# One more column group of a GEGLU layer by seven products, with its LayerNorms moved

## The chip, the core and the metric

The kernel runs on one core of one Trainium2 chip. The metric is the time of one execution on the device in microseconds, the median of several runs. TensorE (PE) multiplies matrices, VectorE (DVE), ScalarE (ACT) and GpSimd (POOL) work element by element, SyncE (SP) issues nearly all DMAs. Each engine takes its own instructions strictly in the order written, and waits where an operand is not there yet.

## The reference

The layer takes `x` (2048 rows of 640) and computes, in float32, attention and a feed-forward part, each behind a LayerNorm and each added to its input:

```
h   = x + attention(layernorm(x))            # 32 heads of 20, window of 256 rows
h2  = h + (gelu(n @ w_gate) * (n @ w_up)) @ w_down      with n = layernorm(h)
```

`w_gate` and `w_up` are 640 x 1536, `w_down` is 1536 x 640. The change concerns the second line alone.

## The kernel before

**Tiling.** The rows are cut into 16 blocks of 128, and for the feed-forward part into four chunks of 512 rows (chunk 0 to 3). The 1536 columns of `w_gate` and `w_up` are cut into three column groups of 512 (group 0 to 2), and a group into four tiles of 128 columns. Every float32 operand is split into two float16 parts, high and low (`hh`, `hl` for the rows; `w5h`, `w5l` and so on for weights: `gu` and w5, w6 hold the gates of groups 0, 1, 2; `gu`, w8, w9 the ups; w10, w11, w12 the downs), and a product of two such operands is three float16 products summed: high by high, high by low, low by high.

**Order of the groups.** `ORDER` (L1061) lists pairs (chunk, group): (0,0), (1,0), (0,1), (0,2), (1,1), (1,2), then the three groups of chunk 2 and of chunk 3. The first `PLAIN` (L1063) pairs are made by `gate_up` (L1104): for each of the four tiles, five contraction steps of three products of 512 columns for the gate, and as many for the up. The result of a tile goes through GELU, is multiplied (`gel`), and split again into `ah` and `al` (`gate_out`, L1087). `down` (L1219) then multiplies the four tiles of a pair by the down weights in eight halves of twelve products of 320 columns, and VectorE adds each half to the accumulator `ht` (`down_out`, L1233). Plain pairs and `down` share two PSUM banks named mm.

**The seven products.** The remaining pairs are made by `quad` (L1135). It shares work between gate and up and between the two halves of 256 rows of a chunk in the manner of a fast matrix multiplication, so that for the low parts seven block products of 128 by 256 do for eight; beside them are the two high-by-high products of 512 columns. It needs sums of the rows (`token_sums`, L1289, twenty VectorE instructions for a chunk, tile `ts` or `wst`) and sums of the weights (`weight_sums`, L1314: for each tile two instructions on POOL and two on VectorE, tile `ws` with two buffers). The weight sums of a group are computed the first time that it is needed, stored to DRAM (`wsums`) and loaded in later chunks (`QLOAD`). A tile takes one bank tp, one of ra, one pv, one of rb, put together by `quad_out` (L1172) on ScalarE, POOL and VectorE. Between two tiles come two halves of the `down` of the pair before.

**Weights.** The feed-forward weights come through one buffer, `wst`, one after another in the order gate, up, down of each group: load, VectorE's maximum, a scale, the split into high and low, and only then the next load.

**LayerNorm.** Chunk 0 is normalised during attention (`first_norm_lane`, L1338) from the block `ht`, into a tile `lxn`, and transposed on TensorE. Chunks 1 to 3 are read back from DRAM (`h_dram`) into two buffers `wsl` by two lanes h and i, a block at a time (`norm_start` and `norm_lane`, L1266 and L1277), normalised there, split, and transposed by DMA into `hT` (`turned`, L499). Chunk 2 uses chunk 0's `hT` tiles and chunk 3 those of chunk 1, so `norm_start` waits until all three groups of the chunk two before have been issued.

**What sets the order.** A planner in the kernel (`Clock`, L54, and the loop at L1561) runs generators called lanes and writes every engine's instructions in the order in which it believes that they become ready, by its own costs; lanes for the outputs of matmuls come ahead of side lanes (weights, sums, LayerNorm), each with a bound on how far ahead it may be written (`FFBACK`, L296). The order on an engine is fixed when the kernel is built. All operations are recorded under one line, L199, so tiles and not lines tell them apart.

Of the kernel before, what the change touches and what calls it, by code (L numbers as in the profile page):

```python
# [11 lines left out]
F32 = mybir.dt.float32  # L12
# [9 lines left out]
S, D, H, DH, F = 2048, 640, 32, 20, 1536  # L22
P = 128
NB = S // P
KC = D // P
# [4 lines left out]
FG = 3  # L30
# [19 lines left out]
def _pow2(e):  # L50
    return float(2.0 ** e)
# [202 lines left out]
def block_kernel(ctx: ExitStack, tc: tile.TileContext, x, wqkv, wo, wg, wu, wd, out):  # L254
    nc = Clock(tc.nc)
# [4 lines left out]
    lnp = ctx.enter_context(tc.tile_pool(name="lnp", bufs=2))  # L260
# [6 lines left out]
    opened, pos = Counter(), Counter()  # L267
# [25 lines left out]
    OUT, PREP, RAMPMAX, FFPREP, LATE = 0.75, 0.55, 0.25, 0.2, 0.4  # L293
# [8 lines left out]
    def need(*reads, slots=(), when=None, eng="tensor"):  # L302

        def f():
            if when and not when() or any(opened[n] >= banks[n] for n in slots):
                return INF
            return max([nc.ready(reads, eng)]
                       + [nc.slot(psum, n, banks[n]) for n in slots])
        return f

    def pe(*reads, slots=(), when=None):
        return ("tensor",), need(*reads, slots=slots, when=when)

    def on(eng, *reads, when=None, after=None):
        f = need(*reads, when=when, eng=eng)
        if after is not None:
            return (eng,), lambda: max(f(), nc.others(after, eng))
        return (eng,), f
# [132 lines left out]
    W = {}  # L451
# [9 lines left out]
    def layernorm(xt, lane, hi, lo, dst=None, when=None, xn=None, e=XE, tp="tp",  # L461
                  dma=False):

        T = lambda n, *shape: nc.tile(lnp, [P] + list(shape), F32, n + lane)
        st = T("lst", 2, 6)
        for i in range(2):
            yield on("vector", xt)
            nc.vector.bn_stats(st[:, i, :], xt[:, i * 320:(i + 1) * 320])
        yield on("vector", st)
        mv = T("lmv", 2)  # L470
        nc.vector.bn_aggr(mv, st)
        yield on("vector", mv)
        ve = T("lve", 1)
        nc.vector.tensor_scalar(ve, mv[:, 1:2], EPS, None, op0=ALU.add)
        yield on("gpsimd", ve)

        y = T("ly", 1)
        a = T("lya", 1)
        nc.gpsimd.tensor_tensor(y, ve, mhalf, op=ALU.pow)
        yield on("vector", y)  # L480
        nc.vector.scalar_tensor_tensor(a, y, ve, y, op0=ALU.mult, op1=ALU.mult)
        yield on("vector", a)
        nc.vector.tensor_scalar(a, a, -0.5 * _pow2(e), 1.5 * _pow2(e), op0=ALU.mult, op1=ALU.add)
        yield on("vector", a)
        nc.vector.tensor_tensor(y, y, a, op=ALU.mult)
        yield on("vector", y)
        xn = xn()
        nc.vector.tensor_scalar(xn, xt, mv[:, 0:1], y, op0=ALU.subtract, op1=ALU.mult)
        if dma:
            yield from turned(xn, lane, (hi, lo), dst, when)  # L490
            return
        yield pe(xn, slots=[tp], when=when)
        if dst:
            hi, lo = dst()
        yield from transpose_part(xn, hi, lo, 0, 4, tp)
        yield pe(xn, slots=[tp])
        yield from transpose_part(xn, hi, lo, 4, 5, tp)
# [84 lines left out]
    gu = ffw.tile([P, 4 * KC * 512], F16, name="gu")  # L582
# [3 lines left out]
    gu = gu.rearrange("p (a c f) -> p a c f", c=KC, f=512)  # L586
# [52 lines left out]
    def hpart(c, b):  # L639
        return tuple(t[:, :, b * P:(b + 1) * P] for t in hT[c])  # L640
# [12 lines left out]
    B = [Block() for _ in range(NB)]  # L653
# [406 lines left out]
    NCH = S // (CB * P)  # L1060
    ORDER = [(0, 0), (1, 0), (0, 1), (0, 2), (1, 1), (1, 2)]  # L1061
    ORDER += [(c, fg) for c in range(2, NCH) for fg in range(FG)]
    PLAIN = 4  # L1063
    hts, ga = {}, {}
    ffpools = [None, None]

# [197 lines left out]
    lnbuf = []  # L1264

    def norm_start(c):  # L1266
        yield ("sync",), need(when=lambda: pos["gu", c - 2] == FG if c > 1 else (
            ffpools[0] and W["d", 0].ready and all(b.wrote for b in B[CB:2 * CB])), eng="sync")
        if c == 1:
            hT[1] = tuple(nc.tile(ffpools[0], [P, KC, CB * P], F16, n) for n in ("h1h", "h1l"))  # L1270
            lnbuf.extend(nc.tile(stage, [P, D], F32, "wsl", SLICES) for _ in range(3))
        else:
            hT[c] = hT[c - 2]
        for i, n in enumerate("hi"):
            side.append((LATE, norm_lane(c, (i, i + 2), n, lnbuf[i])))

    def norm_lane(c, bs, lane, t):  # L1277
        for b in bs:
            j = c * CB + b
            yield ("sync",), lambda: nc.others(t, "sync")  # L1280
            nc.sync.dma_start(t, h_dram[j * P:(j + 1) * P, :])
            yield from layernorm(t, lane, *hpart(c, b), xn=lambda: t, dma=True)
            chunk[c] += 1
        if chunk[c] == CB:
            side.append((LATE, token_sums(c)))
# [3 lines left out]
    def token_sums(c):  # L1289
        hh, hl = hT[c]  # L1290
        h1, h2 = hh[:, :, :CW], hh[:, :, CW:]
        l1, l2 = hl[:, :, :CW], hl[:, :, CW:]
        yield on("vector", when=lambda: ffpools[1] and (c == 1 or W["d", FG - 1].ready))
        t = (nc.tile(ffp, [P, KC, 512], F32, "ts") if c % 2 else
             nc.tile(ffpools[0], [P, KC, 512], F32, "wst")).bitcast(F16)
        t = t.rearrange("p c (a n) -> p a c n", a=4)
        for ks in (slice(k, k + 1) for k in range(KC)):
            a, b, m, d = (t[:, i, ks] for i in range(4))
            yield on("vector", h1, h2)
            nc.vector.tensor_tensor(a, h2[:, ks], h1[:, ks], op=ALU.subtract)  # L1300
            yield on("vector", a, l2)
            nc.vector.scalar_tensor_tensor(b, a, -_pow2(-TE), l2[:, ks], op0=ALU.mult, op1=ALU.add)
            yield on("vector", b, l1)
            nc.vector.tensor_tensor(d, l1[:, ks], b, op=ALU.subtract)
            yield on("vector", l2, h2)
            nc.vector.scalar_tensor_tensor(m, l2[:, ks], _pow2(TE), h2[:, ks], op0=ALU.mult,
                                           op1=ALU.subtract)
        TS[c] = t

    WS = {}  # L1310
    QLOAD = [(c, fg) for c in range(2, NCH) for fg in range(FG) if (c, fg) != (2, 0)]
    wsums = dram.tile([FG * FT, P, 4 * KC * P], F16, name="wsums")

    def weight_sums(c, fg, ft):  # L1314
        kept = wsums[fg * FT + ft]
        t = nc.tile(ffp, [P, 4, KC, P], F16, "ws", 2)
        flat = t.rearrange("p a c f -> p (a c f)")
        if (c, fg) in QLOAD:
            yield ("sync",), need(kept, eng="sync")
# [18 lines left out]
    def first_norm_lane():  # L1338

        for b in range(CB):  # L1340
            yield on("vector", when=lambda: B[b].halves == 2)
            yield from layernorm(B[b].h, "h", *hpart(0, b),
                                 xn=lambda: nc.tile(lnp, [P, D], F32, "lxn"))
            B[b].normed = True
            chunk[0] += 1


    later = [(kind, fg) for fg in range(FG) for kind in "gud"]
# [113 lines left out]
    ffp = None  # L1462
# [5 lines left out]
    def feed_forward():  # L1468
        quads = [(c, fg, ft) for c, fg in ORDER[PLAIN:] for ft in range(FT)]

        def sums_lane():
            for i, q in enumerate(quads):
                yield on("gpsimd", when=lambda: pos["quads"] >= i - 1 and W["d", 2].ready)
                yield from weight_sums(*q)

        side.append((LATE, sums_lane()))
        sums["r", 0] = nc.tile(ffp, [P, 2, CW], F32, "rr")
        sums["r", 1] = nc.tile(ffpools[0], [P, CB * P], F32, "gelt").rearrange(
            "p (a n) -> p a n", a=2)
        sums["s"] = nc.tile(ffp, [P, 3, CW], F32, "rs")  # L1480
        prev = None
        for c, fg in ORDER[1:PLAIN]:
            yield from gate_up(c, fg)
            if prev:
                yield from down(*prev)
            prev = (c, fg)
        for c, fg in ORDER[PLAIN:]:
            groups = down(*prev)

            def fill():  # L1490
                for _ in range(2):
                    for y in groups:
                        if y is None:
                            break
                        yield y

            pool = ffpools[ORDER.index((c, fg)) % 2]
            ga[c, fg] = tuple(nc.tile(pool, [P, FT, CB * P], F16, n) for n in ("ah", "al"))
            for ft in range(FT):
                yield from quad(c, fg, ft, fill)  # L1500
            pos["gu", c] += 1
            prev = (c, fg)
        yield from down(*prev)
# [48 lines left out]
    side = [(LATE, g) for g in lanes]  # L1552
# [91 lines left out]
```

## Time and profile before

| what | before |
|---|---|
| median of three runs | 1042.01 us (1041.12 to 1042.12) |
| profiled execution, its own time | 1043.35 us |
| its span on the core | 1041.6 us |
| TensorE busy | 1019.7 us, 98% of the span |
| VectorE, ScalarE, POOL busy | 778.4, 490.6, 269.8 us |
| granted TensorE clock, mean over the span | 0.996 |

Times in the rows below are microseconds from the start of the span. A row of the chain or of the timeline is start, duration, engine, line, and what was written from what; `x3` is a count, and `[2.00 <-DVE gel L199]` is idle time ahead of the instruction and the one that ended it. A row of a table by stages gives the stage, its length, the busy time of each engine with the count of its instructions, the granted clock, the share of the DMA engines and their rate. Matmuls overlap, so their pace is read from one start to the next.

By the trace, attention ends at about 613 us. Pair (1,0) starts at 619.3, (0,1) at 646.1, `down` of (1,0) at 672.2, (0,2) at 686.0, `down` of (0,1) at 712.5, the first pair by seven products, (1,1), at 729.4. Each of the eight pairs by seven products takes some 37 us together with the `down` work between its tiles; the `down` of the last pair closes the kernel.

### The profile page before, as it was taken

What the parts mean: (1) busy time and instruction counts of PE and PEld (TensorE: products, weight loads), DVE (VectorE), ACT (ScalarE), POOL (GpSimd) and SP (SyncE); (2) the same over time, 40 slices, a digit from 0 to 9 for tenths busy, and PEclk for the clock granted to TensorE, in tenths of its full rate; (3) what the DMA queues carried; (4) which work ended last, traced back from release to release, by engine and by line L of the source; (5) the groups of instructions that cost most, each with busy time, mean ns of one, the idle gap of its engine ahead of it and who ended that gap; (6) DMA issues with size and microseconds to landing.
All of it is one profiled execution on the core that took longest, in us unless ns stands there. A gap on an engine that the chain in (4) does not pass through costs nothing.

```text
span 1041.6 us, 26895 instructions
## 1 busy us (share of the span) xinstructions
PE 1019.7 (98%) x10802; PEld 691.2 (66%) x10802; DVE 778.4 (75%) x2193; ACT 490.6 (47%) x938; POOL 269.8 (26%) x369
## 2 busy tenths in 40 slices
PE   8999999999999999999999899999999999999998
PEld 7876567667666666676655564555777777777776
DVE  6878989998787777677687867676997985445553
ACT  6512667666666766666667835341122222222220
POOL 7100332233333323232323511031445310000000
PEclk9999999999999999999999999999999999999999
DMA  8663354361341513415302341314342652122211
GB/s 300 149 133 114 119 121 132 122 150 55 73 107 43 101 45 77 77 44 112 129 28 90 78 139 52 101 51 127 102 144 110 164 166 77 59 94 102 77 51 51
DMA packets 89116, 105.86 MB, mean 102 GB/s; under 512 B 22176, under 2 KB 63392, under 8 KB 88992
## 3 DMA queue, kind: packets, MB, share of 16 engines
q1 hardware_dynamic: 76896, 93.41, 31.2%
q10 hardware_dynamic: 12096, 10.75, 3.2%
q8 instruction: 84, 1.38, 0.6%
q14 instruction: 40, 0.33, 0.1%
HBM read 71.11 MB, written 28.84 MB: 96 GB/s over the span
## 4 chain that ended last, share of the span: by engine, by line
PE 78%; DVE 13%; issue 3%; DMA 3%; ACT 2%; POOL 0%; SPq 0%; DVEq 0%; ACTq 0%
PE mm L199 40%; PE pv L199 11%; PE ra L199 11%; PE rb L199 9%; PE tp L199 7%; DVE junk L199 4%; DMA qT<-qk 1%; DVE am L199 1%; DMA wst<-in_wd_dram 1%; DVE m L199 1%; DVE al L199 0%; DVE ht L199 0%; ACT pt L199 0%; DVE qks L199 0%; DMA wsl<-h_dram 0%
## 5 line engine op out<-in xcount | busy, mean ns | idle before, releaser
L199 POOL TENSOR_SCALAR_AFFINE_SELECT pt<-pt 128x512 f32<-128x512 f32 x240 | 152.9, 659 | 361.4 <-ACT pt L199 358.7
L199 DVE CUSTOM_DVE_ANT_0 junk<-rb,mask 128x384 bf16<-128x384 f32 (+2 forms) x262 | 138.9, 530 | 42.4 <-PE rb L199 22.6
L199 DVE CUSTOM_DVE_ANT_0 junk<-ra,mask 128x384 bf16<-128x384 f32 (+2 forms) x250 | 132.2, 529 | 41.4 <-PE ra L199 22.3
L199 ACT ACTIVATE pt<-ra,esc 128x384 f32<-128x384 f32 (+2 forms) x248 | 130.7, 579 | 68.4 <-PE ra L199 57.3
L199 ACT ACTIVATE pt<-rb,esc 128x384 f32<-128x384 f32 (+2 forms) x232 | 122.0, 578 | 70.1 <-PE rb L199 59.2
L199 PE MATMUL pv<-pt,v 128*21 128x128 f32 x2880 | 104.8, 277 | 2.1 <-ACT oT L199 2.1
L199 PEld LDWEIGHTS <-ah 128*128 128x128 f16 x768 | 75.5, 98 | 31.1 <-issue 3.1
L199 ACT ACTIVATE gel<-gel,ffk 128x512 f32<-128x512 f32 x32 | 23.1, 722 | 121.4 <-DVE gel L199 121.4
L199 PEld LDWEIGHTS pv<-pt,v 128*21 128x21 f32 x2880 | 68.8, 101 | 17.0 <-ACT oT L199 2.8
L199 PEld LDWEIGHTS <-kT 62*128 62x128 f16 x1440 | 57.8, 95 | 22.7 <-issue 12.7
L199 PEld LDWEIGHTS <-ws 128*128 128x128 f16 x640 | 62.6, 98 | 7.2
L199 PEld LDWEIGHTS <-gu 128*128 128x128 f16 x440 | 42.1, 98 | 36.6 <-issue 1.5
L199 ACT CAST ah<-gel 128x512 f16<-128x512 f32 x48 | 29.6, 616 | 75.7 <-DVE gel L199 75.7
L199 DVE SCALAR_TENSOR_TENSOR ht<-mm,ffk,ht 128x320 f32<-128x320 f32 x96 | 51.9, 545 | 15.9 <-PE mm L199 13.8
L199 PEld LDWEIGHTS <-qT 60*128 60x128 f16 x640 | 24.5, 93 | 56.7 <-issue 55.3
L199 PE MATMUL mm<-xh,w1h 128*128 128x256 f16 x200 | 54.6, 273 | 1.6 <-DVE qks L199 1.6
L199 PE MATMUL mm<-xl,w1h 128*128 128x256 f16 x200 | 54.7, 273 | 0.0
L199 PE MATMUL mm<-xh,w1l 128*128 128x256 f16 x200 | 54.7, 273 | 0.0
L199 PE MATMUL mm<-w3h,oh 128*128 128x320 f16 x160 | 48.0, 300 | 0.1
L199 PE MATMUL mm<-w2h,xh 128*128 128x320 f16 x160 | 48.1, 300 | 0.0
L199 PE MATMUL mm<-w3l,oh 128*128 128x320 f16 x160 | 48.0, 300 | 0.0
L199 PE MATMUL mm<-w2h,xl 128*128 128x320 f16 x160 | 48.0, 300 | 0.0
(296 smaller groups left out, 2531.8 us busy)
## 6 DMA issues: line engine op xcount, KB each, us to landing
ws<-wsums SPq DMA_DIRECT2D x20, 640.0 KB
qk<-qks ACTq DMA_DIRECT2D x32, 256.0 KB
qT<-qk SPq DMA_DIRECT2D x48, 160.0 KB
kT<-qk SPq DMA_DIRECT2D x48, 160.0 KB
wsums<-ws SPq DMA_DIRECT2D x12, 640.0 KB
ht<-in_x_dram SPq DMA_DIRECT2D x16, 320.0 KB
h_dram<-ht SPq DMA_DIRECT2D x16, 320.0 KB
ht<-h_dram SPq DMA_DIRECT2D x16, 320.0 KB
```

Source lines behind the costliest of these rows:

```text
L199: r = real(*args, **kw)
```

## The change

Four edits belong together.

1. `PLAIN` is 3 for 4: pair (0,2) is made by `quad`. Its weight sums (group 2) are now the first to be computed, those of (1,1) come second, and (1,2) loads group 2's from DRAM where it computed them before. Twelve tiles of sums are computed and stored as before; 24 are loaded for 20. The lane of weight sums waits for its own group's gate and up weights, where it waited for the last down weights (`W["d", 2]`).
2. Chunk 0 gets row sums of its own (`token_sums(0)`, tile `ts0`), twenty VectorE instructions, which can start when attention has ended.
3. `norm_start` for chunks 2 and 3 goes when two groups of the chunk two before have been issued, not three: the first block of each of the two lanes is loaded and normalised one group sooner. Only the split and the transposes wait for the third group (`when` in `norm_lane`).
4. The LayerNorm of chunk 0 writes over `ht` itself, and the tile `lxn` goes.

```diff
-    PLAIN = 4
+    PLAIN = 3
...
-        yield ("sync",), need(when=lambda: pos["gu", c - 2] == FG if c > 1 else (
+        yield ("sync",), need(when=lambda: pos["gu", c - 2] == FG - 1 if c > 1 else (
             ffpools[0] and W["d", 0].ready and all(b.wrote for b in B[CB:2 * CB])), eng="sync")
...
-            yield from layernorm(t, lane, *hpart(c, b), xn=lambda: t, dma=True)
+            yield from layernorm(t, lane, *hpart(c, b), xn=lambda: t, dma=True,
+                                 when=lambda: c < 2 or pos["gu", c - 2] == FG)
...
-        yield on("vector", when=lambda: ffpools[1] and (c == 1 or W["d", FG - 1].ready))
-        t = (nc.tile(ffp, [P, KC, 512], F32, "ts") if c % 2 else
+        yield on("vector", when=lambda: ffpools[1] and (c < 2 or W["d", FG - 1].ready))
+        t = (nc.tile(ffp, [P, KC, 512], F32, "ts" if c else "ts0") if c % 2 or not c else
              nc.tile(ffpools[0], [P, KC, 512], F32, "wst")).bitcast(F16)
...
-    QLOAD = [(c, fg) for c in range(2, NCH) for fg in range(FG) if (c, fg) != (2, 0)]
+    QLOAD = [q for i, q in enumerate(ORDER) if q[1] in [fg for _, fg in ORDER[PLAIN:i]]]
...
             yield from layernorm(B[b].h, "h", *hpart(0, b),
-                                 xn=lambda: nc.tile(lnp, [P, D], F32, "lxn"))
+                                 xn=lambda: B[b].h)
             B[b].normed = True
             chunk[0] += 1
+        side.append((LATE, token_sums(0)))
...
-                yield on("gpsimd", when=lambda: pos["quads"] >= i - 1 and W["d", 2].ready)
+                yield on("gpsimd", when=lambda: pos["quads"] >= i - 1 and W["g", q[1]].ready
+                         and W["u", q[1]].ready)
```

## The prediction

> **What bounds the kernel now.** I read the page's busy shares first, then the table by stages, then what TensorE waits for, then the chain, and last the timeline where the chain leaves TensorE.
>
> ```profile
> PE 1019.7 (98%) x10802; PEld 691.2 (66%) x10802; DVE 778.4 (75%) x2193; ACT 490.6 (47%) x938; POOL 269.8 (26%) x369
> ```
>
> TensorE is busy 98% of the span, so what is left to win is a little work and a few waits. The stages show where (span from:to, then busy time of PE, PEld, DVE, ACT, POOL, the granted clock, DMA):
>
> ```profile
> 620.00:646.00 26.00, 25.84 (x122) 11.88 (x121) 19.76 (x49) 11.04 (x17) 2.91 (x3) 1.00 0.32 113
> 646.00:674.00 28.00, 28.00 (x136) 13.22 (x135) 18.59 (x34) 12.52 (x20) 4.60 (x4) 1.00 0.29 95
> 674.00:686.00 12.00, 11.92 (x88) 8.37 (x86) 8.29 (x21) 4.62 (x7) 2.32 (x2) 1.00 0.21 61
> 686.00:716.00 30.00, 28.23 (x136) 13.13 (x135) 20.04 (x34) 9.76 (x14) 9.89 (x7) 1.00 0.24 87
> 716.00:730.00 14.00, 13.71 (x90) 9.46 (x90) 10.78 (x28) 2.07 (x3) 1.10 (x2) 0.88 0.40 95
> 730.00:767.00 37.00, 37.00 (x279) 27.05 (x278) 35.17 (x64) 6.79 (x11) 14.89 (x12) 1.00 0.30 99
> ```
>
> From 730 on TensorE has no idle time: such stages move only if TensorE has less to do. Before, in 686 to 730, it lacks 2.1 us of 44, and in the second of these two stages the granted clock is 0.88, where the other rows have 1.00. The chain passes there through a DMA, and the rows of SP, VectorE and TensorE around it tell the story:
>
> ```profile
> 707.74 4.19 DMA wsl<-h_dram
> ```
> ```profile
> 665.57 2.23 SPq L199 DMA_DIRECT2D wst<-in_wu_dram  x5
> 682.35 2.23 SPq L199 DMA_DIRECT2D wst<-in_wd_dram  x4
> 702.68 5.02 SPq L199 DMA_DIRECT2D wsums<-ws  x2
> 707.74 1.38 SPq L199 DMA_DIRECT2D wsl<-h_dram  x2
> ```
> ```profile
> 711.95 0.89 DVE L199 BATCH_NORM_STATS2 lsth<-wsl 128x6 f32<-128x320 f32 x2 [3.52 <-DMA wsl<-h_dram]
> ...
> 715.50 0.73 DVE L199 SCALAR_TENSOR_TENSOR gel<-mm,ffk,gel 128x512 f32<-128x512 f32 x1
> ```
> ```profile
> 716.29 0.30 PE L199 MATMUL mm<-w11h,ah 128*128 128x320 f16 x1 [2.00 <-DVE gel L199]
> ```
>
> SP issues the load of chunk 2's first row blocks (`wsl`) only behind two stores of weight sums, at 707.74, and it takes 4.19 us. VectorE, in order, stands 3.52 us at the LayerNorm that needs it, so the `gel` that would free one of the two mm banks comes at 715.50, and TensorE stands 2.00 us for it in `down` of (0,1), a short while after pair (0,2) has ended. Then it runs at a lower clock. This incident is the first thing that the change touches.
>
> **The change part by part.**
>
> Pair (0,2) by seven products. Its 120 plain products run from the first of these rows to the third (the second is a maximum of w12, transposed in between); the fourth is where `down` of (0,1) ends. The chain's rows show a tile by seven products with two halves of `down` (from one ra to the next) and the 24 products of those halves:
>
> ```profile
> 686.04 0.38 PE L199 MATMUL mm<-h0h,w6h 128*128 128x512 f16 x1
> ...
> 690.38 0.49 PE L199 MATMUL tp<-ident,am 128*128 128x128 f32 x2
> ...
> 712.50 0.30 PE L199 MATMUL mm<-w11h,ah 128*128 128x320 f16 x1
> ...
> 729.38 0.71 PE L199 MATMUL tp<-h1h,w5l 128*128 128x256 f16 x5
> ```
> ```profile
> 730.63 2.17 PE ra L199 x15
> 733.89 1.63 PE rb L199 x10
> 735.52 3.26 PE mm L199 x24
> 739.87 2.17 PE ra L199 x15
> ```
>
> Plain: 712.50 - 686.04 = 26.46, less some 0.5 us for the maximum, which stays: 25.9 us. By seven products: a tile is 739.87 - 730.63 - 3.26 = 5.98 us, four are 23.9. TensorE has **2.0 us** less to do. All of it counts, as TensorE has no idle time behind it.
>
> The incident. `down` of (0,1) took 712.50 to 729.38, 16.88 us, where 96 products at the pace of 24 in 3.26 are 13.04: **3.84 us** lost, 2.00 by standing and 1.84 behind it, which the clock accounts for (0.12 of 14 us is 1.7). After the change these products lie between the tiles of (0,2), two halves at a time and 5.98 us apart, so a bank that comes free 3.5 us late holds nobody up; and the LayerNorm loads go out when (0,1) has been issued, at about 672, when SP's queue holds no store of weight sums (they begin some 15 us later). I take the whole 3.84 as gained. [...]
>
> What takes its place. The weight sums of (0,2) need the up weights w9, and these are split at the last moment:
>
> ```profile
> 680.88 1.40 DVE L199 SCALAR_TENSOR_TENSOR w9l<-wst,sw,w9h 128x512 f16<-128x512 f32 x2
> ```
> ```profile
> 696.38 1.84 POOL L199 TENSOR_TENSOR ws<-w5l,w8l 128x640 f16<-128x640 f16 x1
> 701.25 1.40 POOL L199 TENSOR_TENSOR ws<-w5h,ws 128x640 f16<-128x640 f16 x1 [3.03 <-DVE ws L199]
> ```
> ```profile
> 700.36 0.81 DVE L199 SCALAR_TENSOR_TENSOR ws<-ws,w8h 128x640 f16<-128x640 f16 x1
> ...
> 701.76 1.57 DVE L199 SCALAR_TENSOR_TENSOR ws<-w8h,w8l 128x640 f16<-128x640 f16 x1
> ```
>
> w9 is complete at 682.28. The first product that needs a sum (`s[:, 1]` in `quad`) has 1280 of a tile's 14,080 columns ahead of it, 0.54 of 5.98 us, so TensorE asks for it at 686.6. From the first POOL start to the end of the second VectorE sum of (1,1)'s first tile it took 701.17 - 696.38 = 4.79 us, with VectorE busy elsewhere in between; bare, by the shortest of these rows, 1.40 + 0.81 + 0.81 = 3.0. Ready at 685.3 to 687.1: the wait is 0 to 0.5 us. The last sum of a tile, POOL's second, takes 1.40 more and is wanted 5120 columns or 2.2 us later, so it follows. The margin is thus used up, where (1,1)'s first tile had 27 us (702.65 to 729.9); every delay of w9 counts in full from here. What can delay it is VectorE's new work ahead of 686:
>
> ```profile
> 613.00:633.00 20.00, 0.00 (x0) 8.41 (x20) 1.00 0.42 148
> ```
> ```profile
> 711.90:715.10 3.20, 2.31 (x8) 1.00 0.02 7
> ```
>
> Twenty row sums cost 8.41 us, and the LayerNorm of one block 2.3 us, two of which (4.6 us) move from behind 707.74 into 672 to 686. Together with the first pair of weight sums (1.6) that is 14.6 us. The stages 620 to 686 leave VectorE 6.2 + 9.4 + 3.7 = 19.3 us idle, so there is room, but in 674 to 686 alone 4.6 + 1.6 meet 3.7. Bounds of the wait at 686: 0, if all fits; 8.9, if the whole row sums pass ahead of the weights (8.4 + 0.5). I take **1.0 us**, as the outputs and the weights' splits are written ahead of sums and LayerNorm. Named cover: idle VectorE. `quad` needs chunk 0's row sums only at 686; they take the place of chunk 1's in the gaps, and chunk 1's are wanted 37 us later.
>
> VectorE in (0,2). The first row is a group in which VectorE has nothing but the tiles and `down`; the second is the work on w12's buffer (maxima and split):
>
> ```profile
> 914.00:951.00 37.00, 37.00 (x279) 27.02 (x277) 19.37 (x37) 7.70 (x12) 2.89 (x4) 1.00 0.28 98
> ```
> ```profile
> 685.00:700.00 15.00, 0.00 (x0) 6.05 (x6) 4.75 (x6) 2.81 (x2) 1.00 0.18 62
> ```
>
> 19.37 + 6.05 and four pairs of weight sums (8 x 0.81) make 31.9 of 37 us. Pair (1,1) had 35.17 in its 37 us without one wait of TensorE (the stage 730 to 767), so I cost this at nothing; without that cover it costs what exceeds 37.
>
> The moved LayerNorms. The two loads of `wsl` leave SP's queue at 707.74 and go behind w9's (665.57), ahead of w12's (682.35). SP is free between 667.8 and 682.35 and w12's load waits there for w9's buffer anyway: nothing. ScalarE's copy and the transposes stay behind the third group, which ends 7 us later than the plain one did; chunk 2 is needed two groups, 74 us, after that: nothing. Chunk 3 lies wholly under TensorE's full stages: nothing.
>
> Sums loaded for computed. Four loads of 640 KB more, four computations less in (1,2), both under a full TensorE: nothing.
>
> LayerNorm in place. VectorE's write must now wait until the store of `ht` has read it.
>
> ```profile
> 236.96 0.33 SPq L199 DMA_DIRECT2D h_dram<-ht  x1
> ```
> ```profile
> 245.00 0.61 DVE L199 TENSOR_SCALAR lxn<-ht,lmvh,lyh 128x640 f32<-128x640 f32 x1
> ```
>
> This is the closest of the four blocks: 8.0 us between the store's issue and the write, while a load of the same 320 KB took 4.19 from issue to use. It costs nothing and gains nothing (it frees a tile of which there was enough); if the store were late, at most its delay beyond 3.9 us.
>
> **The sum**: - 2.0 - 3.84 + 1.0 = - 4.8 us. The profiled execution took 1043.35 us (span 1041.6), which is 1.34 above the median of the runs; it would take 1038.5, and the median 1042.01 becomes **1037.2**.
>
> **The rivals.**
>
> The incident comes back one group earlier. At 672 `down` of (1,0) follows a plain group with the same two banks, and the LayerNorm now falls there. For it: VectorE is in order, and the load may land late behind w9's five pieces. Against: SP is free, and the planner writes outputs first. Price 3.84: 1042.0 - 2.0 - 3.84 + 1.0 + 3.84 = 1041.0.
>
> Slower: the weights come late. One buffer carries them, so each delay by row sums between 613 and 650 (VectorE's maxima, scales, splits) goes on to w9 and from it to 686. TensorE then stands L us and pays 1.84 for the clock; the gain of 5.84 is used up at L = 4.0, and it is slower by over 2.1 from L = 6.1. If all 8.4 us of row sums go ahead, L is 8.9 and the time 1042.0 - 5.84 + 8.9 + 1.84 = 1046.9. For it: no margin at 686. Against: 19.3 us idle. [...]
>
> The change doesn't do what it says: VectorE becomes the bound in (0,2). If the LayerNorms fall into it as well, 31.9 + 4.6 = 36.5, and if each of the eight sums then takes 1.57 for 0.81, 42.6 of 37. TensorE would lose 5.6, and the sum is 1042.0 - 5.84 + 5.6 = 1041.8, no change. [...] Against: pair (1,1), above.
>
> **How the numbers follow.** A measurement of this kernel tells about 0.2% (2.1 us) from no change. Forecast 0.61 (1035.6 to 1039.0: the wait at 686 from 0 to 2.2, and 0.6 for the runs either way); the incident again 0.13 (same); the weights late 0.18 (slower); VectorE the bound 0.08 (same). So faster 0.61, same 0.21, slower 0.18. The range reaches from 1035.4 (no new wait, 1042.01 - 5.84, less 0.8) to 1043.6, which leaves out most of the late weights and little else.
>
> **What would show it.** Right: no matmul of pair (0,2) on mm, its first tile of seven products near 686, the granted clock at 1.00 from 672 to 730, tiles 9.24 apart from there, (2,0) starting some 5 us earlier than now. Wrong: TensorE idle at the first `ts0,ws` for over 2 us, `gel` or `ht` late in 672 to 686, w9's split later than 684, or a tile of (0,2) that takes more than 9.24.

## The result and the profile after

The kernel after takes 1041.62 us in the median of 22 runs (1039.82 to 1042.82); the kernel before took 1042.72 in the runs beside it. The ratio is 0.9986, with a 95% interval of 0.9979 to 0.9992: 1.5 us faster, between 0.8 and 2.2. The forecast was 1037.2 and faster by 4.8. The time lies in the range given, and the direction is right, but two thirds of the gain did not come. Chunk 2 starts 2.8 us earlier in the profiled execution (at 800.45, before at 803.29), not some 5.

The profiled execution took 1040.84 us (span 1038.8). First line: the page's busy shares. TensorE is busy 2.3 us less than before, VectorE 9.2 more.

```profile
PE 1017.4 (98%) x10862; PEld 696.7 (67%) x10862; DVE 787.6 (76%) x2233; ACT 493.0 (47%) x942; POOL 272.0 (26%) x373
```

The stages around the change, cut where the pairs begin and end (columns as in the stages of before):

```profile
646.00:674.00 28.00, 28.00 (x136) 13.16 (x135) 17.96 (x32) 12.40 (x19) 5.10 (x4) 1.00 0.36 117
674.00:686.00 12.00, 10.63 (x77) 7.25 (x75) 11.75 (x37) 5.23 (x8) 3.93 (x5) 1.00 0.01 4
686.00:689.00 3.00, 2.60 (x21) 1.75 (x18) 2.96 (x5) 0.00 (x0) 0.86 (x1) 1.00 0.89 297
689.00:699.00 10.00, 9.27 (x68) 6.68 (x69) 9.96 (x19) 1.71 (x3) 6.78 (x5) 1.00 0.43 171
699.00:726.00 27.00, 27.00 (x204) 19.66 (x203) 23.17 (x40) 10.35 (x16) 15.32 (x12) 1.00 0.19 75
```

Three things are seen. The granted clock is 1.00 in all five stages, and from 699 on TensorE is full: the incident of 712 to 730 is gone. But in 674 to 699, 25 us in which VectorE is busy 24.67, TensorE now lacks 2.50. In 674 to 686 VectorE went from 8.29 to 11.75 us. The timeline of TensorE names the waits:

```profile
675.04 0.49 PE L199 MATMUL tp<-ident,am 128*128 128x128 f32 x2 [0.23 <-DVE am L199]
684.64 0.30 PE L199 MATMUL mm<-w10h,ah 128*128 128x320 f16 x1 [1.09 <-DVE ht L199]
687.89 0.71 PE L199 MATMUL tp<-h0h,w6l 128*128 128x256 f16 x5
689.50 0.72 PE L199 MATMUL tp<-ts,ws 128*128 128x256 f16 x5 [0.90 <-DVE ws L199]
698.82 0.71 PE L199 MATMUL tp<-h0h,w6l 128*128 128x256 f16 x5 [0.23 <-DVE am L199]
726.53 0.71 PE L199 MATMUL tp<-h1h,w5l 128*128 128x256 f16 x5
```

`down` of (1,0) waits 1.09 us for a bank that VectorE's `ht` has not yet read, and the first tile of (0,2) waits 0.90 for its weight sum. What VectorE and POOL were doing, in this order (VectorE first):

```profile
678.10 0.21 DVE L199 SCALAR_TENSOR_TENSOR lyah<-lyh,lveh 128x1 f32<-128x1 f32 x1
...
679.35 1.55 DVE L199 TENSOR_SCALAR wsl<-wsl,lmvh,lyh 128x640 f32<-128x640 f32 x1
...
681.63 1.10 DVE L199 SCALAR_TENSOR_TENSOR lyai<-lyi,lvei 128x1 f32<-128x1 f32 x1 [0.21 <-POOL lyi L199]
682.66 0.74 DVE L199 SCALAR_TENSOR_TENSOR w9l<-wst,sw,w9h 128x512 f16<-128x512 f32 x1
...
684.51 0.74 DVE L199 SCALAR_TENSOR_TENSOR w9l<-wst,sw,w9h 128x512 f16<-128x512 f32 x1
...
685.64 1.90 DVE L199 SCALAR_TENSOR_TENSOR ws<-w9h,w9l 128x640 f16<-128x640 f16 x1
...
687.64 0.61 DVE L199 TENSOR_SCALAR wsl<-wsl,lmvi,lyi 128x640 f32<-128x640 f32 x1
...
688.63 0.81 DVE L199 SCALAR_TENSOR_TENSOR ws<-ws,w9h 128x640 f16<-128x640 f16 x1
```
```profile
677.30 0.55 POOL L199 TENSOR_TENSOR lyh<-lveh,mhalf 128x1 f32<-128x1 f32 x1 [13.83 <-DVE lveh L199]
679.39 1.16 POOL L199 TENSOR_TENSOR w9l<-wst,w9h 128x512 f16<-128x512 f32 x1 [1.54 <-ACT wst L199]
681.04 0.56 POOL L199 TENSOR_TENSOR lyi<-lvei,mhalf 128x1 f32<-128x1 f32 x1 [0.49 <-DVE lvei L199]
681.57 1.16 POOL L199 TENSOR_TENSOR w9l<-wst,w9h 128x512 f16<-128x512 f32 x1
```

The LayerNorm of the two blocks (`lyh`, `lyi`, `wsl`) lies in among the splits of w9. POOL gives its `pow` step `lyi` between its two pieces of w9, and VectorE's LayerNorm instructions fall beside them: `wsl` takes 1.55 us beside POOL's w9 where the other block's, with POOL idle, takes 0.61; the small `lyai` takes 1.10 beside the second piece, where `lyah` took 0.21. So w9 is complete at 685.25, and the first weight sum at 689.44, 4.19 us later. That is the wait of 0.90. (Without the early LayerNorm, in e1 below, the same step takes 3.49 us: the second `wsl` stands in it too.)

### The profile page after: what moved, and what is told of

It reads as the page before. It is cut to its first block, busy times and chain, and to the rows that moved or that the text cites. A ratio compares the mean times of both kernels' runs of the same rounds, so it can differ in the third digit from the quotient of the medians.

```text
span 1038.8 us, 27079 instructions
## 1 busy us (share of the span) xinstructions
PE 1017.4 (98%) x10862; PEld 696.7 (67%) x10862; DVE 787.6 (76%) x2233; ACT 493.0 (47%) x942; POOL 272.0 (26%) x373
## 4 chain that ended last, share of the span: by engine, by line
PE 77%; DVE 13%; issue 3%; ACT 3%; DMA 2%; SPq 1%; POOL 0%; DVEq 0%; ACTq 0%; POOLq 0%
PE mm L199 37%; PE pv L199 12%; PE ra L199 12%; PE rb L199 10%; PE tp L199 7%; DVE junk L199 4%; DVE am L199 1%; DVE ht L199 1%; DVE m L199 1%; DMA ht<-h_dram 1%; ACT pt L199 1%; SPq L199 1%; DMA qT<-in_wqkv_dram 1%; DVE qks L199 1%; DMA wst<-in_wu_dram 0%
## 5 line engine op out<-in xcount | busy, mean ns | idle before, releaser
L199 ACT ACTIVATE gel<-gel,ffk 128x512 f32<-128x512 f32 x36 | 26.0, 722 | 139.4 <-DVE gel L199 139.4
L199 PEld LDWEIGHTS <-ws 128*128 128x128 f16 x720 | 70.2, 98 | 9.4 <-DVE ws L199 1.2
L199 PE MATMUL mm<-w3h,ol 128*128 128x320 f16 x160 | 48.1, 300 | 0.0
```

Source lines behind the costliest of these rows:

```text
L199: r = real(*args, **kw)
```

## The experiments

The theory from this reading: the early LayerNorm is what holds back the gain; it fills VectorE and POOL just while w9 is split. The rivals: chunk 0's row sums, pulled into the same stretch, make the weights late whatever the LayerNorm does; the LayerNorm in place costs something; the LayerNorm's loads, not its work, disturb. And it was open whether the lower clock behind the wait at 716, of which the forecast gained 1.84 us, is in every execution of the kernel before.

To compare single executions, one measure serves for all: how long TensorE took from the first product of `down` of (1,0) to the first of pair (0,2), and from there to the first of pair (1,1). What lies before and after these is alike in all kernels but e7, up to some 2 us between executions at the start (pair (1,0) began anywhere from 618.9 to 621.5); from the first of (1,1) to the end of the span it is 312.2 to 312.3 us in every one, e7 too. Worked out from the timelines of TensorE:

| kernel | `down` of (1,0) | (0,2) to (1,1) | sum | median, us | ratio to before (95%) |
|---|---|---|---|---|---|
| before, five executions of its order (e3, e8, e10, e11 among them) | 13.76 to 14.69 | 41.12 to 43.34 | 55.09 to 57.21, middle 55.56 | 1042.5 to 1042.7 | 1 |
| after | 15.21 | 38.64 | 53.85 | 1041.62 | 0.9986 (0.9979 to 0.9992) |
| e4, after again | 15.44 | 38.62 | 54.06 | 1041.52 | 0.9992 (0.9981 to 1.0002) |
| e1, no early LayerNorm | 14.53 | 37.53 | 52.06 | 1039.13 | 0.9971 (0.9960 to 0.9981) |
| e9, the same again | 14.63 | 37.52 | 52.15 | 1039.89 | 0.9971 (0.9958 to 0.9983) |
| e2, early LayerNorm only | 14.53 | 39.16 | 53.69 | 1040.70 | 0.9986 (0.9971 to 1.0001) |
| e5, early loads, LayerNorm late | 15.37 | 37.53 | 52.90 | 1040.21 | 0.9975 (0.9966 to 0.9984) |
| e6, POOL's step late | 14.42 | 41.73 | 56.15 | 1042.75 | 1.0002 (0.9993 to 1.0012) |

The sums against the middle of before give -1.6 us for the changed kernel (the mean of after and e4), -3.5 for e1, -1.9 for e2, -2.7 for e5, +0.6 for e6. The ratios times 1042.7 give -1.5, -3.0, -1.5, -2.6, +0.2. So the effect of each kernel lies in these 50 us, and the two ways of counting agree within half a microsecond; but each sum is one execution (the changed kernel and e1's have two), and those of before are spread over 2.1 us.

**e1: the change without the early LayerNorm.** Seven products, row sums of chunk 0 and LayerNorm in place stay; the LayerNorms of chunks 2 and 3 start behind the third group again.

```diff
-        yield ("sync",), need(when=lambda: pos["gu", c - 2] == FG - 1 if c > 1 else (
+        yield ("sync",), need(when=lambda: pos["gu", c - 2] == FG if c > 1 else (
...
-            yield from layernorm(t, lane, *hpart(c, b), xn=lambda: t, dma=True,
-                                 when=lambda: c < 2 or pos["gu", c - 2] == FG)
+            yield from layernorm(t, lane, *hpart(c, b), xn=lambda: t, dma=True)
```

> The changed kernel with the start of the LayerNorms of chunks two and three put back to the third group; seven products in (0,2) and the LayerNorm in place stay. Theory (the early LayerNorm does the harm: its two small POOL steps and 4.6 us of VectorE sit between the pieces of w9 and the outputs of down of (1,0)): w9 complete by about 683 and not 685.2, no wait of TensorE at ht before the first tile, at most 0.5 us at the first weight sum; 2 to 2.5 us faster than the changed kernel, 3.5 to 4 faster than before. Rival (chunk 0's row sums, 8.4 us of VectorE, make the weights late): w9 still near 685 and the time within 0.5 us of the changed kernel.

It took 1039.13 us, 2.4 less than the changed kernel on the same chip (e4, 1041.52). Its timeline of TensorE, and the last split of w9 on VectorE:

```profile
685.10 0.30 PE L199 MATMUL mm<-w10h,ah 128*128 128x320 f16 x1 [0.51 <-DVE ht L199]
686.73 0.71 PE L199 MATMUL tp<-h0h,w6l 128*128 128x256 f16 x5
687.27 0.71 PE L199 MATMUL tp<-ts,ws 128*128 128x256 f16 x5
```
```profile
680.89 1.40 DVE L199 SCALAR_TENSOR_TENSOR w9l<-wst,sw,w9h 128x512 f16<-128x512 f32 x2
...
682.68 1.90 DVE L199 SCALAR_TENSOR_TENSOR ws<-w9h,w9l 128x640 f16<-128x640 f16 x1
684.51 0.54 DVE L199 SCALAR_TENSOR_TENSOR ht<-mm,ffk,ht 128x320 f32<-128x320 f32 x1
684.97 0.81 DVE L199 SCALAR_TENSOR_TENSOR ws<-ws,w9h 128x640 f16<-128x640 f16 x1
```

w9 is complete at 682.29, where it was before the change, with chunk 0's row sums in place: the rival of the row sums falls. The first sum is there at 685.78 and wanted at 687.27, with no wait. The tiles start at 686.73, 696.54, 705.78, 715.02: 9.24 apart, as forecast, and only the first is longer, by w12's maximum (0.57). The wait at `ht` did not go, as the expectation had it: 0.51 is left, because the first weight sum, 1.90 us on VectorE, stands ahead of that `ht`. Against before the gain is 3.0 us by the ratio, short of the 3.5 to 4 expected. TensorE has no wait at 717 either, though the LayerNorm loads go out at 717.97: with `down` of (0,1) spread between the tiles, it isn't needed that they come early. The same kernel a second time, on another occasion:

> The kernel of e1 once more, on another occasion: seven products for the one pair more, chunk 0's own row sums and the LayerNorm in place, with the LayerNorm loads of chunks 2 and 3 back behind the third group. If the early LayerNorm is what undoes the gain of the change, this takes 1038.5 to 1040.0 us, ratio 0.996 to 0.998 again, with down of (1,0) to (0,2) about 14.5 us and (0,2) to (1,1) about 37.5. If e1 was a lucky set of runs, the ratio is that of the changed kernel, 0.9985 to 0.9995.

It took 1039.89 with the same ratio. This is the fastest version found, ahead of both kernels.

**e2: the early LayerNorm alone**, in the kernel before (the second and third hunk of the change, nothing else).

```diff
-        yield ("sync",), need(when=lambda: pos["gu", c - 2] == FG if c > 1 else (
+        yield ("sync",), need(when=lambda: pos["gu", c - 2] == FG - 1 if c > 1 else (
...
-            yield from layernorm(t, lane, *hpart(c, b), xn=lambda: t, dma=True)
+            yield from layernorm(t, lane, *hpart(c, b), xn=lambda: t, dma=True,
+                                 when=lambda: c < 2 or pos["gu", c - 2] == FG)
```

> The kernel before with the early LayerNorm alone; (0,2) stays plain. If the incident at 712 (2.0 us of standing, 1.84 of clock) is there in every execution and goes with the load, and the early LayerNorm costs 1.3 us in down of (1,0): 2.5 us faster than before. If the clock's part is there in the profiled execution alone: 0.7 us faster, within what can be told from no change. If the incident only moves to 672: no change.

1040.70 us, ratio 0.9986: 1.5 us faster, between the 2.5 and the 0.7 of the expectation, and no change is just inside the interval. Its timeline of TensorE:

```profile
683.85 0.30 PE L199 MATMUL mm<-w10h,ah 128*128 128x320 f16 x1 [1.09 <-DVE ht L199]
687.11 0.38 PE L199 MATMUL mm<-h0h,w6h 128*128 128x512 f16 x1
...
713.23 0.30 PE L199 MATMUL mm<-w11h,ah 128*128 128x320 f16 x1
...
726.27 0.71 PE L199 MATMUL tp<-h1h,w5l 128*128 128x256 f16 x5
```

From the third row to the fourth `down` of (0,1) takes 13.04 us: without a stall and at full clock, the incident is gone. The 1.09 at `ht` has come, to the hundredth as in the kernel after. w9 is at 684.45, which hurts nobody here, as the plain pair (0,2) wants no sums. So each of the two parts cures the incident by itself. Where both are made, the second cure has nothing left to gain, and its price, the crowded VectorE, stays.

**e3: LayerNorm in place alone.**

```diff
-                                 xn=lambda: nc.tile(lnp, [P, D], F32, "lxn"))
+                                 xn=lambda: B[b].h)
```

> The kernel before with the LayerNorm of chunk 0 in place alone. Theory: no change, within 0.3 us, as the store of a block has 8 us and more before the write over it; the order of the instructions is the same. Rival: VectorE waits for the store; each wait of a microsecond would show at the write into ht, and the time would be over 0.5 us longer.

1042.55 us, ratio 1.0001 (0.9991 to 1.0012): nothing, as forecast. The seven products without this edit were not tried, because the tile `ts0` needs the room that `lxn` leaves.

**e4: the changed kernel again**, in the same series as e1 to e3, for their comparison.

> The changed kernel once more, for a second profile beside the others on the same chip. Theory: the same two waits ahead of the first tile of (0,2) (some 1.1 us at ht, 0.9 at the first weight sum), as they come from the order of instructions; 1 to 1.5 us faster than before. [...]

1041.52 us, with the waits of the first profile (1.09 at `ht`, 0.89 at the first weight sum, 0.22 to 0.28 at two maxima and a `gel`) and w9 at 685.95. By the ratio it is 0.8 us faster than before, with no change inside the interval; only the 22 runs of the first measurement tell the changed kernel clearly from before.

**e5: the loads early, the work late.** As the kernel after, but all of the LayerNorm's work on VectorE waits for the third group.

```diff
-            yield from layernorm(t, lane, *hpart(c, b), xn=lambda: t, dma=True,
-                                 when=lambda: c < 2 or pos["gu", c - 2] == FG)
+            yield on("vector", when=lambda: c < 2 or pos["gu", c - 2] == FG)
+            yield from layernorm(t, lane, *hpart(c, b), xn=lambda: t, dma=True)
```

> The changed kernel, with the first two row blocks of a chunk loaded one group sooner as in it, and the LayerNorm itself put back to the third group. If it is the LayerNorm's work on VectorE and POOL that does the harm: as with the LayerNorms not early at all, w9 complete near 682.3, TensorE's first tile of (0,2) near 686.7, 3 us faster than before. If it is the loads (their traffic behind w9's pieces): w9 near 685, as in the changed kernel, 1 to 1.5 us faster than before.

1040.21 us, ratio 0.9975. TensorE, and the last split of w9 on VectorE:

```profile
687.43 0.30 PE L199 MATMUL mm<-w10h,ah 128*128 128x320 f16 x1 [0.50 <-DVE ht L199]
689.60 0.71 PE L199 MATMUL tp<-ts,ws 128*128 128x256 f16 x5
```
```profile
683.22 1.40 DVE L199 SCALAR_TENSOR_TENSOR w9l<-wst,sw,w9h 128x512 f16<-128x512 f32 x2
```

The loads go out at 669.58, 4.1 us ahead of `down` of (1,0) as in the kernel after (668.58), yet the first weight sum is in time and (0,2) to (1,1) takes the 37.53 of e1; in `down` of (1,0) TensorE waits 0.50 for `ht`, as in e1. (Its other wait there, 0.79 for a maximum, was 0.76 and 0.52 in two executions of the kernel before.) w9 is complete at 684.62, by the number alone nearer to the expectation for harmful loads; but in this execution `down` of (1,0) itself starts 1.5 us later than in e1. Counted from that start w9 comes 10.94 us behind, where e1 has 10.09, after 12.57, and the two executions of before with a wait for the maximum 10.91 and 10.67, without any early load. So the loads do no harm that can be seen; the work does.

**e6: VectorE's statistics early, the rest late.** POOL's `pow` step of the early LayerNorm, and with it what follows, waits until w9 has been split; only the statistics stay early.

```diff
-        yield on("gpsimd", ve)
+        yield on("gpsimd", ve, when=lambda: not dma or pos["gu", 0] < 2 or W["u", 2].ready)
```

> The changed kernel, with the POOL step of the early LayerNorms, and what follows it, held until w9 is split; their statistics on VectorE stay early. If the POOL step between the two POOL pieces of w9 is what makes w9 late: w9 complete by 683.3, against 685.2 to 686.0. If VectorE's 2.4 us of statistics do it: w9 stays later than 684.5. In both cases two POOL steps then stand ahead of the first weight sum, so the wait at it stays near 0.9 us, and the time is between the changed kernel's and that without early LayerNorms.

1042.75 us: the whole gain is gone, where the expectation put the time between the changed kernel's and e1's. Its timeline of TensorE and one of its stages:

```profile
689.83 0.72 PE L199 MATMUL tp<-ts,ws 128*128 128x256 f16 x5 [0.45 <-DVE ws L199]
...
699.49 0.46 PE L199 MATMUL tp<-ident,am 128*128 128x128 f32 x2 [2.02 <-DVE am L199]
```
```profile
686.00:716.00 30.00, 27.53 (x194) 19.53 (x193) 27.23 (x52) 8.87 (x13) 17.23 (x13) 0.94 0.29 110
```

Against `down`'s start w9 is 0.8 us earlier than after (11.76 behind it, for 12.57), but still 1.7 later than in e1 (10.09), so POOL's step between the pieces of w9 explains only a part, and the wait for the sum is halved, not gone. The LayerNorm's remainder now falls on w12's maximum, and TensorE stands 2.02 us there. Behind it the clock is 0.94 over 30 us, 1.8 us of loss. Together, 0.45 + 2.02 + 1.8 is 4.3, and 41.73 less the 37.53 of e1 is 4.20. This profiled execution is the longest of its ten runs (1044.38, the shortest 1040.54), so the part of the clock need not be in each of them; eight of the ten have a mean granted clock of 0.997 or less, against five of the 20 runs of before beside them. In the 25 us from 674 to 699 VectorE is busy 22.50 even in e1, without the LayerNorm, and two blocks of it want 4.6: pushed out of one place it stands in the way at the next.

**e7: one pair more by seven products** (`PLAIN = 2` on e1, so that (0,1) goes by them too).

```diff
-    PLAIN = 3
+    PLAIN = 2
```

> LayerNorms not early, and (0,1) by seven products too, so that ten pairs go so. TensorE has 2.0 us less to do again. If VectorE has room in a group (31.9 of 37 us by the rows): 1.5 to 2 us faster than with nine pairs and no early LayerNorm, 4.5 to 5 faster than before. If VectorE becomes the bound, with weight sums, the weights of groups one and two and chunk 1's row sums all in 646 to 720: TensorE waits at weight sums or at the down weights for more than 2 us, and nothing is gained or the time is longer.

1055.04 us, ratio 1.0117 (1.0101 to 1.0132). The timeline of TensorE and two stages:

```profile
648.50 0.80 PE L199 MATMUL tp<-ident,am 128*128 128x128 f32 x2 [3.74 <-DVE am L199]
...
703.17 1.25 PE L199 MATMUL tp<-ts,ws 128*128 128x256 f16 x5 [7.43 <-DVE ws L199]
```
```profile
646.00:672.00 26.00, 22.93 (x138) 14.55 (x139) 23.57 (x53) 9.09 (x14) 9.87 (x8) 0.87 0.22 77
...
686.00:716.00 30.00, 21.21 (x137) 14.38 (x136) 24.53 (x55) 9.26 (x15) 13.71 (x10) 0.83 0.29 108
```

Here the forecast's slow rival is seen, one pair further on. A maximum of the weights comes 3.74 us late, with VectorE busy 23.57 of 26; w9 is complete only at 700.08, after VectorE itself has stood 1.84 us for ScalarE's part of the split; TensorE stands 7.43 us at the first sum of (0,2), and the clock is lower at both, 0.87 over the first of these stages and 0.83 over the second.

**e8, e10, e11: the kernel before, three more executions.**

> The kernel before, for a second profile. Theory: TensorE again stands 1.9 to 2.0 us in down of (0,1); whether the granted clock falls in the stage behind it differs from one execution to the next, as it did not in the kernel with the LayerNorm in place alone. From the first product of down of (0,1) to the first of (1,1) it is then 15.1 us, or 16.9 with the clock.

> The kernel before, a further look at the wait of TensorE near 717. If the granted clock falls in every execution in which TensorE stands 2 us there, 716 to 730 has 0.88 again and down of (0,1) takes 16.9 us; if it hangs on where the wait falls, the clock is 1.00 in most looks and down takes about 15.2.

> As the look before it: the same order of instructions, so the wait near 717 is 1.9 to 2.1 us; the clock behind it is 0.88 if the wait alone lowers it, and 1.00 in most executions if it hangs on where the wait falls.

The stage 716 to 730 in each (e8, e10, e11), with TensorE's wait at its start 2.04, 1.80 and 1.81 us:

```profile
716.00:730.00 14.00, 12.77 (x96) 9.34 (x96) 12.29 (x32) 2.86 (x5) 1.10 (x2) 1.00 0.47 104
```
```profile
716.00:730.00 14.00, 12.84 (x96) 9.39 (x96) 12.30 (x32) 2.94 (x5) 1.10 (x2) 1.00 0.50 104
```
```profile
716.00:730.00 14.00, 13.76 (x101) 9.86 (x101) 11.92 (x32) 2.65 (x4) 1.50 (x3) 1.00 0.50 111
```

The granted clock, the third number from the end, is what counts: 1.00 in all three, as in e3 (wait 1.90), whose order of work in this stretch is that of before. The 0.88 on which the forecast built was in one of five executions. `down` of (0,1) took 15.24, 15.00 and 15.00 us in these three and 15.10 in e3, so the incident is usually worth 2.0 to 2.2 us, not 3.84. The mean clocks of the other runs fit that. In the profiled execution the loss is a stretch at a clock of 0.50, 3.4 us from 716.8 to 720.3, which costs half its length, 1.7 us; a row from inside it:

```profile
717.00:720.00 3.00, 3.00 (x13) 1.66 (x11) 2.15 (x6) 0.00 (x0) 0.11 (x1) 0.50 0.65 124
```

Worked out from 1.7 of some 1041 us, one such stretch takes the mean over the span to 0.998 and two take it to 0.997. Of the 30 runs of before beside e1, 19 have 0.998 or more, which by this estimate is one stretch at most; and they lie elsewhere too: e4, e8, e10 and e11 have 0.997 or 0.998 with 1.00 in every stage from 620 to 767, while in attention one runs from 122.9 to 126.3 us in the profiled execution of before and one from 123.6 to 130.4 in that of after, and the stage 50 to 140 has 0.98 in e6 and e8.

## Why the prediction came out as it did

Two terms of the sum failed, and one was missing. Of the 3.84 us for the incident, the 1.84 of the clock are not in most executions; the new wait, taken as 1.0, cost 1.9 to 2.2, as the early LayerNorm got in among the splits of w9; and `down` of (1,0) pays 0.5 for the first weight sum, which the sum has at nothing. Together that is 3.2 to 3.5 us, where 3.3 of the forecast 4.8 did not come.

- **Seven products take 2.0 us off TensorE: right.** e1's tiles are 9.24 apart, and no matmul of (0,2) goes to mm. With w12's maximum, which costs 0.57 among these tiles and some 0.2 in the plain pair of e2, it is 1.6: (0,2) to (1,1) takes 39.16 in e2 and 37.53 in e1, both without a wait and at full clock. (The fall of TensorE's busy time in the page, 2.3, is no measure of it, as the half-clock stretch of before is counted as busy.)
- **The incident, -3.84: the mechanism right, the size wrong.** The wait at 716 is gone in after, e1 and e2. Its standing part, 2.00, is real in all five executions (1.80 to 2.04). "I take the whole 3.84 as gained" failed in the other part: the 1.84 of the clock was in the profiled execution and in none of four others. The prediction had the warning in its own sum. That execution took 1.34 us more than the median of the runs, and this extra was carried over to the time after as if it were spread elsewhere, while it was, as far as the traces tell, for the most part the very loss that the change was credited with removing: the half-clock stretch costs 1.7, and the 57.21 of the table is 1.65 over the middle. With the standing part alone the sum would have come out at 1039.0 (1037.2 and the 1.84), which is nearer. And the sum credits the change with one cure for the wait, where e1 and e2 show two, either of them enough.
- **The new wait at 686, +1.0: mis-sized, and one half unseen.** The prediction named the shape rightly: no margin, w9's delay counting in full, two LayerNorms meeting 3.7 us of VectorE's idle time. Its value was taken near the lower bound "as the outputs and the weights' splits are written ahead of sums and LayerNorm". That was the step that failed. The LayerNorm was written among the splits, on POOL too, which the prediction's count of VectorE alone left out; w9 came 3.0 us later, 2.5 when counted from the start of `down` of (1,0). The cost is 0.90 at the sum, 0.23 at the next maximum, and 1.3 (after) to 1.6 (e4) in `down` of (1,0), of which e1 has 0.51 as well. That makes 1.9 to 2.2 us; by the table, e1 against after and e4 is 1.8 to 2.0, and by the medians of one series 2.4. "TensorE idle at the first `ts0,ws` for over 2 us" did not occur, but "`gel` or `ht` late in 672 to 686", "w9's split later than 684" and "a tile of (0,2) that takes more than 9.24" (the first, 10.93) did.
- **Row sums, VectorE in (0,2), sums loaded for computed: nothing, right.** w9 stands at 682.29 in e1, and TensorE is full from 699 on in the kernel after. **LayerNorm in place: nothing, right** (e3), though the remark that there was enough of `lxn`'s room was wrong.
- **The rivals.** The first, the LayerNorm colliding one group earlier, is nearest to what came: "VectorE is in order" was the sound part of it, but the price was 1.1 us of standing and no fall of the clock, not 3.84; the loads had landed in good time. The weights came late as in the second, from the LayerNorm and not from the row sums, by too little to make the kernel slower. VectorE as the bound in (0,2) did not come; with one pair more (e7) VectorE is busy 24.53 of 30 us there, but TensorE's longest wait is for weights that come late.
- **The sum as measured**: -1.6 to -2.0 for the products, -2.0 to -2.2 for the incident, and +0.5 in `down` of (1,0), which e1, e5 and e9 show alike, is -3.1 to -3.7 for e1 (table -3.5, ratio -3.0); with the early LayerNorm's 1.8 to 2.0 it is -1.1 to -1.9 for the changed kernel (table -1.6, ratio -1.5).

What stays open is how the early LayerNorm's harm divides between VectorE's statistics, POOL's step and the lengthened instructions. e6 shows that POOL's step between the pieces of w9 is not all of it; the other two were not tried alone.

## What to carry to other kernels

Before a loss is counted as gained, look at whether it is in more than one execution; when the profiled one is over the median, ask first whether that excess is the loss in question. When two parts of a change cure the same wait, try each alone: here one of them brought a gain of its own and the other cost 2 us. And work moved into a stretch in which a chain of weights has no slack needs room on every engine of that chain, in order, at that place; idle time summed over a longer stretch is no cover.

## What the runs showed of the hardware

- **Behind waits of about 2 us the granted clock fell in some executions and not in others.** At one place and one order, waits of 1.80, 1.81, 1.90 and 2.04 (e10, e11, e3, e8) left it at 1.00 over 716 to 730, and behind one of 2.00 (before) it was 0.88. In e6 it was 0.94 over the 30 us from 686 to 716, with a wait of 2.02 in them. Both are one stretch of 3.4 us at half clock, a loss of 1.7 us each by its length. That of e6 runs from 700.3 to 703.7; a row from inside it:

```profile
700.50:703.50 3.00, 3.00 (x15) 1.95 (x13) 2.75 (x9) 1.47 (x3) 0.62 (x1) 0.50 0.54 218
```

  The stretch of before at 122.9 is 3.4 us long too, that of after at 123.6 is 6.8, and the 0.87 over 26 us and the 0.83 over 30 us of e7 come to 6.8 and 10.2 us at half clock (an estimate from the means). What sets the wait of 2.00 apart from the 2.04 of e8, behind which the clock stayed at 1.00, was not shown, and five cases at this place are few.
- **VectorE beside POOL.** In after, the same LayerNorm instruction of 128x640 took 1.55 us beside POOL's split of w9 and 0.61 with POOL idle; a scalar one of 128x1 took 1.10 beside it, where that of the other block took 0.21. In before, a weight sum of 128x640 (`ws<-w8h,w8l`) took 1.57 us at 701.76, with POOL at its own sum from 701.25, and 0.81 at 699.63, with POOL idle.
